# Mask and maximum of the scores: result written back to PSUM instead of a scratch tile, and both projection copies on ScalarE

## The chip, the cores and the metric

The kernel runs on one core of a Trainium2 chip. The metric is device time in microseconds for one execution of the whole program. The core has TensorE (PE, matmuls from SBUF into PSUM), VectorE (DVE), ScalarE (ACT), GpSimd (POOL) and SyncE (SP), which issues the DMAs. Each engine works through its own queue in order; semaphores order the engines against each other, and, where an instruction touches what an earlier one of the same engine wrote, also an engine against itself.

## The reference

Four layers alternate on x of 2048 rows and 640 columns: attention, Fourier, attention, Fourier. Each is applied to a layer-normalised x and added to x.

```python
def _A_ref(x, wqkv, wo):
    H = 32; Dh = D // H; W = 256
    q, k, v = ...                          # x @ wqkv, 32 heads of 20
    scores = einsum("bhqd,bhkd->bhqk", q, k) * (Dh ** -0.5)
    mask = (i - j >= 0) & (i - j < W)      # causal, a window of 256
    p = softmax(where(mask, scores, -1e9))
    return einsum("bhqk,bhkd->bhqd", p, v) @ wo
def _B_ref(x, ...):                        # real part of a 2-D DFT
    return dft_seq_re @ (x @ dft_hid_re.T) - dft_seq_im @ (x @ dft_hid_im.T)
```

All of it is float32.

## The kernel before

fp32 products are made from fp32r matmuls: each operand is split into a high part (a rounded copy) and a low part (the rest), and three products hi·hi, hi·lo, lo·hi are summed in PSUM. Splitting is what ScalarE, VectorE and GpSimd do most of the time.

An attention layer projects q and k in 10 chunks of 128 rows by 2048 columns, stores them to DRAM, and loads them back packed, four heads (a quad) at a time, into `qp` and `kp`. There are 8 quads of 16 blocks of 128 queries. `heads` walks over 128 head steps and a lead-in of 10. In a step s, t and v are three points of a pipeline that stand 10 steps and one step apart:

- `s_head` (L546): for a block of queries and each of four heads, one matmul gives the scores of 128 queries against up to 384 keys (128 in the first block of a quad, 256 in the second). The scores go to one of three PSUM banks (2, 3, 4) in turn. One VectorE instruction adds the mask to them and takes each row's maximum, which lands in a column of `mc`. The chip runs it as two instructions: the custom operation over the scores and an accumulator read that writes `mc`. Its element-wise result, masked scores, is used by nobody.
- `m_rows` (L561): every four steps the maxima are transposed, negated and stored as a 61st row of `qp`.
- `t_head` and `t_exp` (L574, L581): the scores again, transposed (keys by queries), with that 61st row subtracting the maximum, into bank 0 or 1; ScalarE takes the exponential into `pt`. `t_mask` on GpSimd zeroes what the mask excludes.
- `pv` (L600): the product with v into bank 5, one step later.

Between the two halves of a step `fill` puts other TensorE work: first the projection of the remaining chunks (`project`, `pieces`), then parts of the output product. `pieces` multiplies two sets of 512 columns in lockstep into banks 6 and 7 (in the lead-in four, with 0 and 1 as well). When a set is complete, `copied` (L470) brings each of its banks to an SBUF tile `x`; before the change the odd one goes by VectorE (L474), the even one by ScalarE (L476). GpSimd then rounds and subtracts (L477, L478) in the following half steps, and SyncE stores. The copies are issued at the end of `fill` (L685), so in each queue they stand ahead of the second half of the step.

The order is written out by the program: nothing reorders it. Only the semaphores are derived, from which tile or bank an instruction reads and writes.

Of the kernel before, what the change touches and what calls it, by code (L numbers as in the profile page):

```python
# [9 lines left out]
BF16 = mybir.dt.bfloat16  # L10
U16 = mybir.dt.uint16
AF = mybir.ActivationFunctionType
# [5 lines left out]
P = 128  # L18
# [9 lines left out]
NEG = -1.0e30  # L28
# [33 lines left out]
class Net:  # L62
    def __init__(self, nc, tc, ctx, a):
        self.nc, self.tc, self.a = nc, tc, a
        const = ctx.enter_context(tc.tile_pool(name="const", bufs=1))
        self.ln = ctx.enter_context(tc.tile_pool(name="ln", bufs=5))
        self.slots = ctx.enter_context(tc.tile_pool(name="slots", bufs=1))
        psum = ctx.enter_context(tc.tile_pool(name="psum", bufs=1, space=PSUM))
        self.work = ctx.enter_context(tc.tile_pool(name="work", bufs=2))
        dram = ctx.enter_context(tc.tile_pool(name="dram", bufs=1, space=DRAM))  # L70

        self.banks = psum.tile([P, 8, 512], F32, name="banks")

        def fixed(name, cols, dt):
            return const.tile([P, cols], dt, name=name)

        self.ident = fixed("ident", P, F32)
        nc.sync.dma_start(self.ident, a["ident"])
        self.mask = fixed("mask", 384, BF16)
        self.ux = fixed("ux", 384, BF16)  # L80
        self.ones = const.tile([1, 128], F32, name="ones")
        nc.vector.memset(self.ones, 1.0)
        self.half = fixed("half", 1, F32)
        nc.vector.memset(self.half, -0.5)
        self.big, self.home = [None] * 4, [0, 1, 2, 3]
        self.qp, self.kp = [None] * 2, [None] * 2

        self.qk = dram.tile([2, 2 * D, S], F32, name="qk_d")
        self.vd = dram.tile([NQ, P, NB, 96], F32, name="v_d")
        self.ud = dram.tile([2, KC, P, S], F32, name="u_d")  # L90
        self.od = dram.tile([H, 32, S], F32, name="o_d")
        self.rd = dram.tile([NSB, H, 512], F32, name="r_d")
        self.xs = [dram.tile([S, D], F32, name=f"x_d{i}") for i in range(3)]
        self.turn = {}
        self.xn = {}
        self.ready, self.hid = 0, False
        self.slot = None
        self.posted = {}
        self.heavy = []
        self.left = 0  # L100
        self.tmp = None
# [355 lines left out]
    def pieces(self, c, sbs, role):  # L457

        w = self.turn["w", c]
        sets, of = [], {}  # L460
        for sb in sbs:
            xt = self.xnt(sb)
            if sb % 2 == 0:
                sets.append(([], []))
            p = self.bank(role)
            of[id(p)] = p, sb, self.last_bank
            sets[-1][0].append(p)
            sets[-1][1].append([((w[:, 0, k, :], w[:, 1, k, :]), (xt[:, 0, k, :], xt[:, 1, k, :])) for k in range(KC)])

        def copied(p, sb):  # L470
            st = self.work.tile([P, 2, 512], F32R, name="c", tag="c", bufs=3)
            r = self.raw()[:, :512]
            if sb % 2:
                self.nc.vector.tensor_copy(r, p)  # L474
            else:
                self.nc.scalar.activation(r, p, AF.Copy)  # L476
            self.post(1, lambda: self.nc.gpsimd.tensor_copy(st[:, 0, :], r))  # L477
            self.post(2, lambda: self.nc.gpsimd.tensor_tensor(  # L478
                out=st[:, 1, :], in0=r, in1=st[:, 0, :].bitcast(F32), op=OP.subtract))
            self.post(6, lambda: self.store_qk(c, sb, st))  # L480
        for r in self.lockstep(sets):
            if isinstance(r, tuple):
                for p in r[1]:
                    p, sb, k = of[id(p)]
                    self.heavy.append((k, lambda p=p, sb=sb: copied(p, sb)))
                r = 0
            yield r
# [33 lines left out]
    def heads(self, xsrc, xdst, hook):  # L521
# [20 lines left out]
        def s_bank():  # L542
            turn[0] += 1
            return 2 + turn[0] % 3

        def s_head(quad, qb, z, e):  # L546

            n = min(qb + 1, 3)
            k0 = qb - n + 1
            b = 64 * e  # L550
            p = self.banks[:, s_bank(), :n * P]
            nc.tensor.matmul(  # L552
                p, qp[quad % 2][b:b + 60, z, qb * P:(qb + 1) * P],
                kp[quad % 2][b:b + 60, z, k0 * P:(qb + 1) * P], start=True, stop=True)
            if (quad, qb // 4) not in mc:
                mc[quad, qb // 4] = pool.tile([P, 2, 2, 4], F32, name="mc", tag="mc")
            nc.vector.tensor_tensor_reduce(  # L557
                out=self.ux[:, :n * P], in0=p, in1=self.mask[:, 384 - n * P:], scale=1.0, scalar=NEG,
                op0=OP.add, op1=OP.max, accum_out=mc[quad, qb // 4][:, z, e, qb % 4:qb % 4 + 1])

        def m_rows(quad, u):  # L561
# [128 lines left out]
        for step in range(-LEAD, steps + 1):  # L690
# [24 lines left out]
            for z in range(2):  # L715
                for e in range(2):
                    heads = [(t_head, t, e), (s_head, s, 1 - e)]
                    for head, n, i in heads[::-1] if e else heads:
                        if 0 <= n < steps:
                            head(n // 16, n % 16, z, i)  # L720
                if 0 <= t < steps:
                    for e in range(2):
                        t_exp(t // 16, t % 16, z, e, e + 1)
                    t_mask(t // 16, t % 16, z)
                if z:
                    if 0 <= v < steps:
                        pv(v // 16, v % 16)
                    if rows:
                        m_rows(*rows)
                if z == 0 and t >= 0 or t < -1 or t >= steps:  # L730
                    fill(nf)
                self.tick()
# [798 lines left out]
```

## Time and profile before

| what | value |
|---|---|
| median of 3 runs | 2284.34 us (2281.37 to 2285.37) |
| profiled execution | 2282.01 us, of it the span 2280.3 us |
| mean granted TensorE clock | 0.989 |
| PE busy | 2185.6 us (96%) |
| VectorE busy | 1512.0 us (66%) |
| ScalarE busy | 1106.0 us (49%) |
| GpSimd busy | 1004.1 us (44%) |
| score matmuls (L552), first and last start, first attention layer | 124.5 and 521.4 us |
| the same, second attention layer | 1255.8 and 1651.9 us |
| mask-and-maximum (L557) | 1024 instructions, 545.1 us busy, mean 532 ns; 186.5 us of idle VectorE ahead of them |

Busy time is a share of stretches with different limits, so the head steps have to be read by themselves. A matmul's end is modelled and matmuls overlap, so a PE that is busy all the time need not be at its peak; idle time of the weight loads (PEld) tells more. A wait is put down to the semaphore that came last.

### The profile page before, as it was taken

Reading aid. Unit: us, or ns where it says so; the run is one execution under the profiler, and the core shown is the slowest. Engines: PE = TensorE matmul, PEld = TensorE weight load, DVE = VectorE, ACT = ScalarE, POOL = GpSimd, SP = SyncE. Lnnn points to the kernel's source line nnn. Section 1 sums busy time; section 2 is a strip of 40 time slices with the busy share of each in tenths; the row PEclk is TensorE's granted clock in tenths of the full one; section 3 lists DMA queues with packets and bytes.
Section 4 is the critical chain, followed back from the end, with each engine's and each line's share of the span. In section 5 each row is a group of like instructions: output and inputs, shape, how many; then the busy total and the mean of one; then the engine's idle time right before and its main releaser. Section 6 shows DMA issues by size and latency. Waiting matters only on the chain.

```text
span 2280.3 us, 50212 instructions
## 1 busy us (share of the span) xinstructions
PE 2185.6 (96%) x18064; PEld 1811.8 (79%) x18064; DVE 1512.0 (66%) x3737; ACT 1106.0 (49%) x2369; POOL 1004.1 (44%) x1540
## 2 busy tenths in 40 slices
PE   8999999999889999999999999998998899999999
PEld 7976777677768888889999777766777688888999
DVE  6357777774787868772451677776746978688622
ACT  2117776666454545541331377676655545445310
POOL 3037666777743223230130566668777332332300
PEclk9999999999989999999999999999999999999999
DMA  5545656775435353655455456657654354446553
GB/s 188 179 148 181 182 175 193 226 208 162 139 116 177 121 184 130 219 173 166 153 170 182 153 184 176 192 179 227 198 174 129 115 171 148 160 151 207 165 167 99
DMA packets 217305, 385.64 MB, mean 169 GB/s; under 512 B 38880, under 2 KB 85472, under 8 KB 217056
## 3 DMA queue, kind: packets, MB, share of 16 engines
q1 hardware_dynamic: 217056, 382.43, 52.7%
q8 instruction: 143, 2.34, 0.4%
q14 instruction: 106, 0.87, 0.1%
HBM read 267.39 MB, written 113.77 MB: 167 GB/s over the span
## 4 chain that ended last, share of the span: by engine, by line
PE 36%; POOL 5%; DVE 4%; DMA 2%; issue 2%; ACT 1%; SPq 0%; DVEq 0%; POOLq 0%; ACTq 0%
PE banks L1224 14%; PE banks L171 11%; PE banks L189 4%; PE banks L607 3%; DVE ux L557 2%; PE banks L577 2%; PE banks L552 2%; POOL big L164 1%; POOL c L478 1%; POOL pt L592 0%; POOL pt L596 0%; DMA rr<-r_d 0%; POOL kp L164 0%; POOL x L773 0%; DMA kp<-qk_d 0%
## 5 line engine op out<-in xcount | busy, mean ns | idle before, releaser
L557 DVE CUSTOM_DVE_ANT_0 ux<-banks,mask 128x384 bf16<-128x384 f32 (+2 forms) x1024 | 545.1, 532 | 186.5 <-PE banks L552 53.0
L586 ACT ACTIVATE pt<-banks 128x384 f32<-128x384 f32 (+2 forms) x1024 | 435.8, 469 | 223.2 <-PE banks L552 118.5
L577 PE MATMUL banks<-qp,kp 61*128 61x384 f32 (+2 forms) x1024 | 329.7, 383 | 8.9 <-ACT pt L586 8.5
L552 PE MATMUL banks<-kp,qp 60*128 60x384 f32 (+2 forms) x1024 | 313.3, 377 | 19.5 <-DVE mc L557 18.8
L592 POOL TENSOR_SCALAR_AFFINE_SELECT pt<-pt 128x256 f32<-128x256 f32 x512 | 210.2, 411 | 224.3 <-ACT pt L586 185.9
L189 PE MATMUL banks<-big,wc 64*128 64x512 f32 x1920 | 263.0, 391 | 0.4 <-DVE pt L372 0.4
L577 PEld LDWEIGHTS banks<-qp,kp 61*128 61x128 f32 x1024 | 179.4, 185 | 68.9 <-ACT pt L586 40.0
L552 PEld LDWEIGHTS banks<-kp,qp 60*128 60x128 f32 x1024 | 172.8, 185 | 74.8 <-DVE mc L557 61.6
L607 PE MATMUL banks<-pt,vq 128*32 128x128 f32 x5760 | 217.2, 278 | 7.8 <-POOL pt L592 7.8
L164 DVE TENSOR_TENSOR qp<-pt,qp 128x512 fp32r<-128x512 f32 (+1 forms) x209 | 173.2, 837 | 50.0 <-ACT qp L158 49.0
L189 PEld LDWEIGHTS banks<-big,wc 64*128 64x128 f32 x1920 | 184.3, 186 | 20.4 <-DVE pt L372 0.5
L607 PEld LDWEIGHTS banks<-pt,vq 128*32 128x32 f32 x5760 | 144.2, 110 | 61.9 <-issue 46.7
L596 POOL TENSOR_SCALAR_AFFINE_SELECT pt<-pt 128x256 f32<-128x256 f32 x448 | 184.2, 411 | 0.0
L158 ACT ACTIVATE qp<-pt 128x512 fp32r<-128x512 f32 (+1 forms) x209 | 128.9, 624 | 102.4 <-DMA pt<-c 35.3
L1224 PE MATMUL banks<-qp,big 128*128 128x512 f32 x630 | 156.2, 399 | 6.1 <-POOL big L164 4.3
L1153 POOL TENSOR_TENSOR pt<-pt,pt 128x512 f32<-128x512 f32 x40 | 58.5, 1466 | 214.0 <-DMA pt<-c 162.4
L1412 DVE TENSOR_TENSOR x<-banks,x 128x320 f32<-128x320 f32 x64 | 29.8, 488 | 178.4 <-DMA x<-x_d 103.1
L1224 PEld LDWEIGHTS banks<-qp,big 128*128 128x128 f32 x630 | 120.3, 193 | 32.6 <-POOL big L164 5.8
L158 ACT ACTIVATE c<-pt 128x512 fp32r<-128x512 f32 x144 | 88.1, 624 | 75.7 <-DVE pt L1150 37.3
L171 PE MATMUL banks<-big,pt 128*128 128x320 f32 x768 | 118.2, 309 | 0.9 <-DVE pt L1349 0.9
L1224 PE MATMUL banks<-qp,xc 128*128 128x512 f32 x480 | 119.0, 395 | 0.0
L164 DVE TENSOR_TENSOR c<-pt,c 128x512 fp32r<-128x512 f32 x140 | 107.9, 783 | 15.1 <-ACT c L158 12.7
(202 smaller groups left out, 4395.3 us busy)
## 6 DMA issues: line engine op xcount, KB each, us to landing
pt<-c SPq DMA_DIRECT2D x188, 512.0 KB
qk_d<-c SPq DMA_DIRECT2D x80, 512.0 KB
kp<-qk_d SPq DMA_DIRECT2D x384, 80.0 KB
qp<-qk_d SPq DMA_DIRECT2D x384, 80.0 KB
kp<-u_d SPq DMA_DIRECT2D x32, 640.0 KB
o_d<-ou SPq DMA_DIRECT2D x64, 256.0 KB
x_d<-x SPq DMA_DIRECT2D x48, 320.0 KB
v_d<-pt SPq DMA_DIRECT2D x16, 768.0 KB
```

What stands on the lines that cost most here:

```text
L158: nc.scalar.activation(hi, src, AF.Copy, scale=-1.0 if neg else 1.0)
L164: (eng or nc.vector).tensor_tensor(out=lo, in0=src, in1=hi.bitcast(F32), op=OP.subtract)
L171: self.nc.tensor.matmul(p, x, y, start=n == 0, stop=n == last)
L189: self.nc.tensor.matmul(ps[a], x[r], y[r], start=half + i == 0, stop=half == 1 and i == n - 1, skip_group_check=True)
L552: nc.tensor.matmul(p, qp[quad % 2][b:b + 60, z, qb * P:(qb + 1) * P], kp[quad % 2][b:b + 60, z, k0 * P:(qb + 1) * P], start=True, stop=True)
L557: nc.vector.tensor_tensor_reduce(out=self.ux[:, :n * P], in0=p, in1=self.mask[:, 384 - n * P:], scale=1.0, scalar=NEG, op0=OP.add, op1=OP. ...
L577: nc.tensor.matmul(self.banks[:, e, :n * P], kp[quad % 2][b:b + 61, z, kb * P:(kb + 1) * P], qp[quad % 2][b:b + 61, z, kb * P:(kb + n) * P ...
L586: nc.scalar.activation(pt[quad, kb][:, 2 * z + e0:2 * z + e1, :n * P], self.banks[:, e0:e1, :n * P], AF.Exp, scale=SCALE)
L592: nc.gpsimd.affine_select(out=t[:, :, 0:P], in_=t[:, :, 0:P], pattern=[[0, 2], [1, P]], compare_op=OP.is_ge, fill=0.0, base=0, channel_mul ...
L596: nc.gpsimd.affine_select(out=t[:, :, 256:384], in_=t[:, :, 256:384], pattern=[[0, 2], [-1, P]], compare_op=OP.is_gt, fill=0.0, base=0, ch ...
L607: nc.tensor.matmul(p[32 * h:32 * h + 32, :], vq[:, 96 * (kb % 4) + 21 * h:96 * (kb % 4) + 21 * h + 32], t[:, h, (qb - kb) * P:(qb - kb + 1 ...
L1224: nc.tensor.matmul(self.banks[:, bk, :], p, b[q], start=start and m == 0, stop=stop and last and m == 2, skip_group_check=True)
```

## The change

The element-wise result of the mask-and-maximum goes back to the bank that holds the scores (in place, as fp32) instead of to `ux`, a bf16 tile in SBUF that all 1024 shared; the tile is gone. In `copied` both copies go by ScalarE.

```diff
         self.mask = fixed("mask", 384, BF16)
-        self.ux = fixed("ux", 384, BF16)
...
             r = self.raw()[:, :512]
-            if sb % 2:
-                self.nc.vector.tensor_copy(r, p)
-            else:
-                self.nc.scalar.activation(r, p, AF.Copy)
+            self.nc.scalar.activation(r, p, AF.Copy)
...
             nc.vector.tensor_tensor_reduce(
-                out=self.ux[:, :n * P], in0=p, in1=self.mask[:, 384 - n * P:], scale=1.0, scalar=NEG,
+                out=p, in0=p, in1=self.mask[:, 384 - n * P:], scale=1.0, scalar=NEG,
                 op0=OP.add, op1=OP.max, accum_out=mc[quad, qb // 4][:, z, e, qb % 4:qb % 4 + 1])
```

VectorE in the steady head steps, around one projection copy, before. Rows `ISA ux,mc` are the mask-and-maximum, rows `ISA mc` its accumulator read; in brackets stand the semaphores that an instruction waits for, by the engine that raises them (DVE is VectorE's own).

```order
L557 ISA ux,mc<-banks,mask 128x384 [waits DVE_49,PE_49]
L557 ISA mc 128x1
L557 ISA ux,mc<-banks,mask 128x384 [waits DVE_49,PE_49]
L557 ISA mc 128x1
L474 COPY x<-banks 128x512 [waits PE_49,Pool_49]
L557 ISA ux,mc<-banks,mask 128x384 [waits DVE_49,PE_49,Activation_49]
L557 ISA mc 128x1
L557 ISA ux,mc<-banks,mask 128x384 [waits DVE_49,PE_49]
```

The same place after the change, where the lines are four lower:

```order
L553 ISA banks,mc<-banks,mask 128x384 [waits PE_49]
L553 ISA mc 128x1
L553 ISA banks,mc<-banks,mask 128x384 [waits PE_49]
L553 ISA mc 128x1
L553 ISA banks,mc<-banks,mask 128x384 [waits PE_49,Activation_49]
L553 ISA mc 128x1
L553 ISA banks,mc<-banks,mask 128x384 [waits PE_49]
```

The copy is gone from VectorE's queue, and with `ux` the wait of each mask-and-maximum for its own engine; the wait for TensorE stays.

ScalarE at a copy of the same kind, before. L586 are the exponentials, four to a step, two in each half; L616 and L566 bring products and maxima out of PSUM, L158 rounds weights.

```order
L616 ACTIVATE ou_98<-banks 128x256
L566 ACTIVATE mt<-banks 16x128
L586 ACTIVATE pt_97<-banks 128x384 x2
L476 ACTIVATE x<-banks 128x512
L586 ACTIVATE pt_97<-banks 128x384 x2
L586 ACTIVATE pt_94<-banks 128x384 x2
L158 ACTIVATE wc<-x 128x384
```

And after:

```order
L612 ACTIVATE ou_97<-banks 128x256
L562 ACTIVATE mt<-banks 16x128
L582 ACTIVATE pt_96<-banks 128x384 x2
L472 ACTIVATE x<-banks 128x512 x2
L582 ACTIVATE pt_96<-banks 128x384 x2
L582 ACTIVATE pt_93<-banks 128x384 x2
L157 ACTIVATE wc<-x 128x384
```

Two copies now stand between the exponentials of the first and the second half of that step. The order of TensorE, GpSimd and SyncE is what it was; in 6 places, three in each lead-in, a projection matmul gains a wait for ScalarE, where VectorE's copy had been covered by a wait of an earlier matmul.

## The prediction

> **What bounds the kernel now.** I read the page first, then busy time in stretches of the span, then the list of waits, then the order of time on VectorE, ScalarE and TensorE inside two head steps.
>
> ```profile
> span 2280.3 us, 50212 instructions
> ```
>
> Busy time by stretch: the stretch, its length, then busy us and count of instructions of each engine, the granted clock, the DMA share.
>
> ```profile
> core 0: us, PE busy (x) PEld busy (x) DVE busy (x) ACT busy (x) POOL busy (x), PEclk, DMA share, GB/s
> 125.00:160.00 35.00, 34.76 (x308) 28.34 (x309) 21.26 (x77) 3.65 (x8) 13.54 (x16) 1.00 0.39 123
> 200.00:240.00 40.00, 39.03 (x535) 28.59 (x533) 30.90 (x117) 27.81 (x69) 27.05 (x61) 1.00 0.62 192
> ...
> 800.00:1180.00 380.00, 377.80 (x2061) 338.50 (x2060) 237.10 (x387) 154.04 (x267) 97.16 (x77) 1.00 0.53 174
> ```
>
> The first row is the lead-in of the head steps, the second a steady part of them, the third the Fourier layer, which the change does not touch. In the steady part PE looks full, yet its weight loads are busy for 28.6 of 40 us against 338.5 of 380 in the Fourier layer: PE waits there between a load and its matmul. The list of waits names for whom:
>
> ```profile
> PEld banks L552 <- DVE mc L557: 61.6, 175, 1.0
> ...
> PE banks L552 <- DVE mc L557: 18.8, 63, 0.8
> ```
>
> The score matmul (L552) waits for the mask-and-maximum (L557) to give a PSUM bank back. The next fence is VectorE in order of time in two steady head steps (start us, length us):
>
> ```profile
> 302.98 0.56 DVE L557 CUSTOM_DVE_ANT_0 ux<-banks,mask 128x384 bf16<-128x384 f32 x1
> 303.46 0.08 DVE L557 DVE_READ_ACCUMULATOR2_ANT mc<- 128x1 f32 x1
> 303.46 0.25 DVE L630 RECIPROCAL rc<-sm 128x16 f32<-128x16 f32 x1
> 303.69 0.56 DVE L557 CUSTOM_DVE_ANT_0 ux<-banks,mask 128x384 bf16<-128x384 f32 x1
> 304.17 0.08 DVE L557 DVE_READ_ACCUMULATOR2_ANT mc<- 128x1 f32 x1
> 304.40 0.56 DVE L557 CUSTOM_DVE_ANT_0 ux<-banks,mask 128x384 bf16<-128x384 f32 x1
> ```
>
> One mask-and-maximum starts every 0.71 us (303.69, 304.40). Its accumulator read starts after 0.48 us, and from there 0.23 us pass before the next one. In that hole a RECIPROCAL of 0.25 us fits without moving the next start, so VectorE could have worked; it was waiting. Four of them make 2.84 us a step.
>
> One quad of steady steps, cut at the first transposed matmul (L577) of its steps 0, 1, 2, 3, 4 (to 5), 6, 7 (to 9), 10, 11, 12 (to 13), 14 (to 15); columns as above:
>
> ```profile
> 302.88:305.50 2.62, 2.62 (x45) 2.02 (x41) 2.24 (x8) 1.69 (x4) 0.93 (x3) 1.00 0.45 145
> 305.50:307.89 2.39, 2.39 (x29) 1.61 (x25) 1.87 (x8) 1.86 (x6) 1.54 (x4) 1.00 0.65 170
> 307.89:311.14 3.25, 3.19 (x37) 2.05 (x33) 2.62 (x9) 2.23 (x6) 1.54 (x4) 1.00 0.61 195
> 311.14:314.34 3.20, 2.93 (x39) 2.08 (x38) 2.77 (x10) 2.48 (x7) 1.85 (x5) 1.00 0.14 42
> 314.34:320.83 6.49, 6.10 (x84) 4.37 (x80) 4.99 (x20) 4.92 (x12) 6.49 (x12) 1.00 0.59 177
> 320.83:323.66 2.83, 2.83 (x43) 2.20 (x41) 1.68 (x10) 1.81 (x5) 2.83 (x8) 1.00 0.97 355
> 323.66:331.53 7.87, 7.87 (x119) 6.00 (x118) 5.76 (x22) 6.00 (x15) 4.60 (x13) 1.00 0.55 157
> 331.53:334.46 2.93, 2.93 (x45) 2.08 (x41) 2.35 (x10) 1.88 (x6) 1.63 (x5) 1.00 0.72 155
> 334.46:337.42 2.96, 2.69 (x39) 1.95 (x38) 2.53 (x10) 2.47 (x7) 1.72 (x5) 1.00 0.18 60
> 337.42:343.14 5.72, 5.72 (x84) 4.23 (x80) 4.71 (x18) 4.24 (x10) 5.72 (x11) 1.00 0.70 219
> 343.14:349.10 5.96, 5.68 (x83) 4.22 (x79) 4.76 (x18) 2.85 (x10) 2.66 (x8) 1.00 0.75 264
> ```
>
> Where VectorE has slack (step 0, and 7 to 9, after the narrow instructions of 128 and 256 columns) a step takes 2.62 us: TensorE's own pace. Elsewhere three things stretch it. VectorE does in steps 2, 10, 14 and 15. GpSimd is busy 6.49 of 6.49, 2.83 of 2.83 and 5.72 of 5.72 us in steps 4 to 6 and 12 to 13, where it cuts the projection pieces. The copies fall in steps 3 and 11. So VectorE paces only a part of what it makes others wait for.
>
> **The change part by part.** The rows for its prices:
>
> ```profile
> L557 DVE CUSTOM_DVE_ANT_0 ux<-banks,mask x1024: 280/558/560, 125.1 to 1653.4; 128x384 bf16<-128x384 f32 x149, 128x128 bf16<-128x128 f32 x11, 128x256 bf16<-128x256 f32 x11
> ...
> L557 DVEq EVENT_SEMAPHORE  x1022: 21/21/1487, 125.4 to 1653.3; - x171
> ...
> L1150 DVE TENSOR_TENSOR pt<-pt 128x512 f32<-128x512 f32 x60 | 42.1, 702 | 0.0
> ...
> L474 DVE COPY x<-banks x32: 685/689/693, 136.6 to 1559.9; 128x512 f32<-128x512 f32 x32
> ...
> L476 ACT ACTIVATE x<-banks x32: 597/598/601, 136.6 to 1559.8; 128x512 f32<-128x512 f32 x32
> ```
>
> *The scratch tile goes, and a wait with it.* All 1024 instructions wrote the one tile `ux`, so each waited for the one before it on its own engine; 1022 extra semaphore instructions carried that wait. Written into the scores' own bank the outputs no longer overlap, and the wait on TensorE alone is left. The next one may then start where the RECIPROCAL did, at the accumulator read: 0.48 us instead of 0.71, four in 1.93 us. VectorE falls clear of the 2.62 us of TensorE, and more saving on it would buy nothing.
>
> *The output goes to PSUM as fp32.* No row shows VectorE writing PSUM. The nearest rows show reading: a 512-column copy out of PSUM takes 689 ns, an operation of that width within SBUF 702. From below I bound the price at nothing (0 ns, no gain either, since the columns are streamed anyway); from above at a second pass over the columns. A pass costs (558 - 280) / 256 = 1.09 ns a column, so 0.42 us for 384, and 0.90 us from start to start. I take the lower end, since as a source PSUM is no slower than SBUF.
>
> *The copies.* 32 of 689 ns leave VectorE, 32 of 598 ns come to ScalarE. Eight lie in the lead-in, where ScalarE is busy 3.65 of 35 us. There the change adds six waits of projection matmuls (with all of TensorE's queue behind them) for ScalarE. Between a set's end and the next use of its banks lies the other set:
>
> ```profile
> 136.59 1.99 PE L189 MATMUL banks<-big,wc 64*128 64x512 f32 x16
> ...
> 138.59 1.77 PE L189 MATMUL banks<-big,wc 64*128 64x512 f32 x14
> ```
>
> That is 3.8 us, and two copies end 1.2 us after their set. So I cost it at nothing; were that cover gone, it would be at most 0.6 us in each of six places, 3.6 in all. The other 24 stand right behind the 24 that are there, in steps 3 and 11, with two exponentials of the same step queued after them. Step 11 now: ScalarE, TensorE, VectorE:
>
> ```profile
> 336.42 0.60 ACT L476 ACTIVATE x<-banks 128x512 f32<-128x512 f32 x1 [0.18 <-PE banks L189]
> 336.92 0.87 ACT L586 ACTIVATE pt<-banks 128x384 f32<-128x384 f32 x2
> ...
> 336.22 0.34 PE L577 MATMUL banks<-qp,kp 61*128 61x384 f32 x1
> ...
> 337.45 0.44 PE L577 MATMUL banks<-qp,kp 61*128 61x384 f32 x1
> ...
> 336.53 0.69 DVE L474 COPY x<-banks 128x512 f32<-128x512 f32 x1
> ```
>
> The scores of 336.22 are there at 336.56, but their exponential starts at 336.92, behind the copy, and ends about half of 0.87 us later, just before the next transposed matmul at 337.45 needs its bank. Another 0.60 us of copy puts that matmul 0.60 later. Nothing covers it, so steps 3 and 11 come to 2.62 + 0.60 = 3.22 us. GpSimd's cutting of the second piece waits for its copy, which ends at 337.6 either way (336.87 + 0.69, or 336.42 + 1.20); GpSimd's full stretches stay.
>
> *The sum for one quad* (46.22 us now): step 2 gives 3.25 - 2.62 = 0.63, step 10 gives 0.31, steps 14 and 15 give 5.96 - 5.24 = 0.72. In steps 12 and 13 GpSimd is full but TensorE shows no idle time (5.72 of 5.72), so I take half of 5.72 - 5.24, 0.25. Step 3 stays, step 11 costs 0.26, the rest stays. Together 1.65 us.
>
> ```profile
> PEld banks L552 <- DVE mc L557: 19.2, 60, 0.5
> ...
> 455.96:459.90 3.94, 3.67 (x53) 2.76 (x52) 2.62 (x11) 2.25 (x8) 3.80 (x6) 1.00 0.92 226
> ...
> 462.98:467.29 4.31, 3.65 (x56) 2.76 (x52) 2.87 (x11) 2.65 (x6) 4.31 (x8) 1.00 0.78 202
> ```
>
> The first row is the same wait between 205.0 and 446.7 us, 5.2 quads: 3.7 us each. So 1.65 of 3.7, 45%, comes back. The later head steps, filled with output products, are alike: the long ones (3.94 and 4.31 us) have GpSimd busy 3.80 and 4.31. I apply the 45% to all 61.6 us: 28 us. The profiled execution took 2282.0 us (2280.3 span, 1.7 around it), 2.3 below the median of 2284.3; 2282.0 - 28 = 2254, from the median 2256. I say 2255.
>
> **The rivals.**
>
> *All of the wait returns.* GpSimd's full stretches could be a backlog that shrinks when masks come earlier, and ScalarE's second copy could slide into its gaps. For it: ScalarE is busy 27.8 of 40 us. Against it: the three stretches at 100%. Time: 2282 - 61.6 = 2220.
>
> *The hole stays.* VectorE may need the time to finish an instruction, wait or no wait. The RECIPROCAL at 303.46 speaks against it, though it is another operation than the one that would follow now. Then only copies leave VectorE, at most 0.6 us in each of 24 places where ScalarE costs about the same: 0 to -7 us, 2279. The Trainium skill says this in "VectorE: DVE Perf Modes", section "The DRAIN you can't avoid": the next operation starts only when the pipe is empty, and eight copies took 13.88 us with a semaphore after each and with one after the last alike. By that rule the sum would be 2279; the trace disagrees with it in the row at 303.46, and I leave it a chance for that reason only.
>
> *Slower: PSUM takes the write at half pace.* At 0.90 us a start, a quad has 14 steps of 3.6, one of 4 x 0.63 and one of 4 x 0.34 (the 256- and 128-column forms with their second pass): 54.3 us on VectorE alone, 8.1 more than 46.2. Seven such quads in each of two layers: +113, so 2395. The point from which it decides is a start-to-start time of 0.71 us, 0.23 more than now lies between a start and its accumulator read. Nothing in the trace shows a PSUM operand doing that.
>
> **How the numbers follow.** The forecast has 0.57, all the wait 0.20, the hole that stays 0.13, slower 0.10. The likeliest gives 2255. The range takes in the two middle rivals, 2220 to 2281, and leaves the slow one out. About 0.2% (4.6 us) is what a measurement can tell from no change; the rival of the hole straddles it. So faster 0.83, the same 0.07, slower 0.10.
>
> **What would show it.** Right: mask-and-maximum starts 0.48 us apart when scores are ready; the semaphore instructions of that line down from 1022 to some tens; the 61.6 us wait under 15; steps 2, 10, 14 and 15 at 2.6 us; 64 copies of 598 ns on ScalarE, and the transposed matmul waiting for exponentials in steps 3 and 11. Wrong: a start-to-start time still at 0.71 (the hole stays), an instruction near 0.98 us long (the PSUM write), steps 4 to 6 shorter than 9.3 us together (GpSimd was no bound, and the gain is larger), or a granted clock under 1.00 in 200 to 400 us as TensorE fills up.

## The result, and the profile after

The changed kernel takes 2262.28 us (median; 2256.79 to 2264.44) against 2284.64 us before (2281.37 to 2285.37) on the same chip: a ratio of 0.9901, with a 95% interval of 0.988 to 0.9923, or 22 us less. The forecast was 28 us less. The profiled execution took 2260.54 us.

The mask-and-maximum and the copies, by line (duration ns as least/median/most):

```profile
span 2258.8 us, 49233 instructions
...
L553 DVE CUSTOM_DVE_ANT_0 banks<-banks,mask x1024: 289/567/602, 126.6 to 1633.5; 128x384 f32<-128x384 f32 x149, 128x128 f32<-128x128 f32 x11, 128x256 f32<-128x256 f32 x11
L553 DVE DVE_READ_ACCUMULATOR2_ANT mc<- x1024: 133/141/146, 126.8 to 1634.0; 128x1 f32 x171
L553 DVEq EVENT_SEMAPHORE  x58: 21/21/21, 176.1 to 1624.4; - x58
...
L472 ACT ACTIVATE x<-banks 128x512 f32<-128x512 f32 x64 | 34.7, 595 | 55.6 <-PE banks L188 24.1 <-POOL wc L163 17.8 <-issue 12.5
```

VectorE in order of time in a steady head step (start us, length us):

```profile
300.67 0.57 DVE L553 CUSTOM_DVE_ANT_0 banks<-banks,mask 128x384 f32<-128x384 f32 x1
301.15 0.14 DVE L553 DVE_READ_ACCUMULATOR2_ANT mc<- 128x1 f32 x1
301.15 0.60 DVE L553 CUSTOM_DVE_ANT_0 banks<-banks,mask 128x384 f32<-128x384 f32 x1
```

The hole is gone: the next mask-and-maximum starts at the accumulator read of the one before, 0.48 us after its start (300.67, 301.15) instead of 0.71. The semaphore instructions fell from 1022 to 58. Writing fp32 to PSUM shows in two durations: the accumulator read takes 141 ns instead of 83, beside the next instruction, and the instruction itself 567 instead of 558 (medians). Neither moves the next start. What TensorE waits for:

```profile
PEld banks L573 <- ACT pt L582: 43.9, 141, 0.8
...
PEld banks L548 <- DVE mc L553: 23.6, 51, 3.0
...
PE banks L548 <- DVE mc L553: 10.7, 17, 2.7
```

The waits of the score matmul for the mask-and-maximum fell from 61.6 and 18.8 us to 23.6 and 10.7. Its longest grew from 1.0 to 3.0; that one comes up again below.

Now the steady quad, cut at its steps as in the prediction (2, 3, 4 to 5, 6, 10, 11, 12 to 13, 14 to 15 are shown):

```profile
303.87:306.77 2.90, 2.90 (x34) 2.21 (x34) 2.55 (x10) 2.05 (x6) 1.53 (x4) 1.00 0.71 212
306.77:309.82 3.05, 2.69 (x39) 1.94 (x39) 2.64 (x11) 2.85 (x9) 2.28 (x6) 1.00 0.37 117
309.82:316.03 6.21, 5.88 (x81) 4.50 (x82) 4.60 (x17) 4.92 (x12) 6.12 (x11) 1.00 0.56 169
316.03:318.85 2.82, 2.82 (x43) 2.17 (x41) 1.21 (x8) 1.81 (x5) 2.82 (x8) 1.00 1.01 376
...
326.73:329.57 2.84, 2.84 (x45) 2.15 (x41) 2.48 (x10) 1.87 (x6) 1.54 (x5) 1.00 0.61 172
329.57:332.46 2.89, 2.70 (x40) 1.92 (x39) 2.43 (x11) 2.81 (x8) 2.10 (x6) 1.00 0.13 39
332.46:337.91 5.45, 5.45 (x80) 4.35 (x80) 4.31 (x16) 4.13 (x10) 5.45 (x10) 1.00 0.69 216
337.91:342.98 5.07, 5.07 (x83) 4.03 (x80) 4.44 (x17) 2.90 (x11) 2.66 (x8) 1.00 0.92 320
```

Steps 2, 4 to 5, 12 to 13 and 14 to 15 are shorter; steps 3 and 11, with two copies on ScalarE, still take 3.05 and 2.89. This quad takes 44.1 us instead of 46.2. All quads of the two attention layers, as quad 0, quads 1 to 4, quads 5 to 7; before:

```profile
161.25:209.67 48.42, 44.83 (x590) 32.19 (x589) 36.92 (x136) 32.17 (x79) 34.40 (x73) 1.00 0.65 206
209.67:395.75 186.08, 180.55 (x2452) 131.02 (x2448) 145.16 (x536) 130.20 (x320) 126.24 (x281) 1.00 0.59 183
395.75:550.88 155.13, 146.49 (x2091) 113.96 (x2088) 102.25 (x358) 102.34 (x247) 114.44 (x219) 0.98 0.67 195
1291.89:1339.89 48.00, 44.82 (x590) 32.15 (x590) 36.92 (x136) 32.17 (x79) 34.40 (x73) 1.00 0.65 207
1339.89:1525.59 185.70, 180.69 (x2453) 131.20 (x2450) 145.06 (x536) 130.36 (x320) 126.00 (x280) 1.00 0.60 183
1525.59:1681.11 155.52, 146.15 (x2091) 114.02 (x2087) 102.31 (x358) 102.51 (x247) 114.76 (x219) 0.98 0.65 195
```

And after:

```profile
162.81:210.74 47.93, 44.75 (x589) 33.49 (x588) 35.66 (x135) 32.85 (x81) 34.25 (x73) 0.96 0.63 206
210.74:387.05 176.31, 172.38 (x2453) 132.38 (x2450) 141.10 (x529) 131.62 (x328) 125.98 (x281) 1.00 0.61 189
387.05:545.93 158.88, 149.82 (x2091) 116.96 (x2088) 100.79 (x356) 102.96 (x249) 114.46 (x219) 0.95 0.67 195
1284.11:1330.74 46.63, 43.40 (x590) 32.65 (x590) 35.66 (x135) 32.68 (x81) 34.35 (x73) 1.00 0.67 209
1330.74:1506.89 176.15, 172.26 (x2453) 132.34 (x2449) 141.10 (x529) 131.54 (x328) 125.97 (x281) 1.00 0.62 193
1506.89:1661.90 155.01, 148.43 (x2092) 116.02 (x2088) 100.58 (x356) 103.03 (x249) 114.44 (x219) 0.96 0.67 196
```

Of 21.5 us of span, quads 1 to 4 give 9.8 and 9.6, quad 0 gives 0.5 and 1.4, and 3.6 lie outside the quads. Quads 5 to 7 give nothing: +3.75 and -0.5. So there are three questions: what the PSUM result and the copies are each worth, what holds the steps that did not come down to 2.62 us, and why the late quads gained nothing.

### The profile page after: what moved, and what is told of

It is laid out like the page before. It is cut to its first block, busy times and chain, and to the rows that moved or that the text cites. A ratio compares the mean times of both kernels' runs of the same rounds, so it can differ in the third digit from the quotient of the medians.

```text
span 2258.8 us, 49233 instructions
## 1 busy us (share of the span) xinstructions
PE 2169.5 (96%) x18064; PEld 1817.8 (80%) x18064; DVE 1489.8 (66%) x3705; ACT 1114.2 (49%) x2401; POOL 1014.9 (45%) x1540
## 3 DMA queue, kind: packets, MB, share of 16 engines
q8 instruction: 143, 2.34, 0.5%
## 5 line engine op out<-in xcount | busy, mean ns | idle before, releaser
L553 DVE CUSTOM_DVE_ANT_0 banks<-banks,mask 128x384 f32<-128x384 f32 (+2 forms) x1024 | 526.7, 557 | 174.7 <-PE banks L548 125.7
L582 ACT ACTIVATE pt<-banks 128x384 f32<-128x384 f32 (+2 forms) x1024 | 430.8, 469 | 209.4 <-PE banks L548 115.0
L573 PE MATMUL banks<-qp,kp 61*128 61x384 f32 (+2 forms) x1024 | 320.0, 376 | 10.7 <-ACT pt L582 9.2
L548 PE MATMUL banks<-kp,qp 60*128 60x384 f32 (+2 forms) x1024 | 285.5, 367 | 11.4 <-DVE mc L553 10.7
L163 DVE TENSOR_TENSOR qp<-pt,qp 128x512 fp32r<-128x512 f32 (+1 forms) x209 | 167.7, 811 | 50.8 <-ACT qp L157 50.0
L548 PEld LDWEIGHTS banks<-kp,qp 60*128 60x128 f32 x1024 | 164.8, 188 | 32.9 <-DVE mc L553 23.6
L553 DVE DVE_READ_ACCUMULATOR2_ANT mc<- 128x1 f32 x1024 | 144.9, 141 | 0.0
```

The lines of the kernel that those rows point to most:

```text
L163: (eng or nc.vector).tensor_tensor(out=lo, in0=src, in1=hi.bitcast(F32), op=OP.subtract)
L548: nc.tensor.matmul(p, qp[quad % 2][b:b + 60, z, qb * P:(qb + 1) * P], kp[quad % 2][b:b + 60, z, k0 * P:(qb + 1) * P], start=True, stop=True)
L553: nc.vector.tensor_tensor_reduce(out=p, in0=p, in1=self.mask[:, 384 - n * P:], scale=1.0, scalar=NEG, op0=OP.add, op1=OP.max, accum_out=mc ...
L573: nc.tensor.matmul(self.banks[:, e, :n * P], kp[quad % 2][b:b + 61, z, kb * P:(kb + 1) * P], qp[quad % 2][b:b + 61, z, kb * P:(kb + n) * P ...
L582: nc.scalar.activation(pt[quad, kb][:, 2 * z + e0:2 * z + e1, :n * P], self.banks[:, e0:e1, :n * P], AF.Exp, scale=SCALE)
```

## The experiments

Theory: the gain is the own-engine wait on the scratch tile; the copies on ScalarE give part of it back in steps 3 and 11; GpSimd holds what is left. Rivals: it is the target PSUM that counts, or the copies pay for themselves. Each time below is a median; the ratio behind it is to runs of the kernel before on the same chip.

### One part at a time

The PSUM result alone, with the copies as before (the diff without its part in `copied`).

> Only the result goes back to PSUM; the two copies stay on VectorE and ScalarE as before. My theory (the wait on VectorE's own engine made the hole, and the second copy on ScalarE costs time in steps 3 and 11): mask-and-maximum 0.48 us apart as with the whole change, steps 3 and 11 at 2.7 instead of 3.05 and 2.87 us, so about 10 us less than the whole change, 2252. Rival (taking copies off VectorE was half of the gain): 2273.

Measured: 2256.85 us, 0.9892 (0.9878 to 0.9906). Quads 1 to 4 take 43.67 us on average.

The copies alone (the diff's part in `copied`, nothing else).

> Only the copies move to ScalarE; the scratch tile stays. My theory: mask-and-maximum still 0.71 us apart, VectorE gains 0.6 us in 24 places and TensorE waits longer for exponentials in the same steps: 2280, between 2274 and 2286. Rival (the copies were half of the gain): 2273.

Measured: 2282.28 us, 0.9995 (0.9986 to 1.0004). The copy steps 3 and 11, with the PSUM result alone:

```profile
303.20:305.82 2.62, 2.62 (x40) 1.95 (x39) 2.41 (x8) 2.43 (x8) 1.85 (x5) 1.00 0.31 96
...
325.86:328.48 2.62, 2.62 (x39) 1.91 (x39) 2.22 (x10) 2.54 (x7) 1.85 (x5) 1.00 0.15 55
```

and with the copies alone:

```profile
311.54:315.22 3.68, 3.00 (x41) 2.08 (x40) 2.93 (x11) 2.96 (x8) 2.35 (x6) 1.00 0.16 48
335.09:338.54 3.45, 2.76 (x39) 1.93 (x38) 2.71 (x9) 2.96 (x8) 2.22 (x6) 1.00 0.29 96
```

The PSUM result carries the whole gain. With one copy on each engine steps 3 and 11 come down to TensorE's 2.62 us; two on ScalarE keep them above it in both kernels. By its steady quads the change would have done better without its second half: they take 44.06 us on average with it, 0.39 more than without. That is 3 us in eight quads, and the times themselves do not tell the two kernels apart (0.9901 and 0.9892, with overlapping intervals).

### Is it PSUM, or the wait?

The copies as in the change, but the result stays in SBUF, and in quads 0 to 4 two tiles alternate, so that no instruction overwrites what the one just ahead of it wrote:

```diff
+            ux = self.rr[2].bitcast(BF16) if quad < 5 and e else self.ux
             nc.vector.tensor_tensor_reduce(
-                out=self.ux[:, :n * P], ...
+                out=ux[:, :n * P], ...
```

> Copies on ScalarE; the result goes to SBUF as before, but in the first five quads of each attention layer to two tiles in turn (ux and rr), so that no instruction has to wait for the one just before it; the last three quads have ux alone. My theory: the wait is the cause, PSUM only the means: starts at most 0.55 us apart in those five quads and steady quads of 44.0 to 44.3 us as with the whole change (before 46.2), accumulator reads of 83 ns instead of 141; from the sixth quad on as before; in all 2262 to 2268. Rival (VectorE starts early only because it writes to PSUM): 0.71 us apart, quads of 46, 2280.

Measured: 2262.39 us, 0.9914 (0.9901 to 0.9928), as the change. VectorE, and the semaphore instructions of that line:

```profile
300.52 0.56 DVE L555 CUSTOM_DVE_ANT_0 rr<-banks,mask 128x384 bf16<-128x384 f32 x1 [0.24 <-PE banks L575]
301.00 0.08 DVE L555 DVE_READ_ACCUMULATOR2_ANT mc<- 128x1 f32 x1
301.00 0.55 DVE L555 CUSTOM_DVE_ANT_0 ux<-banks,mask 128x384 bf16<-128x384 f32 x1
...
L555 DVEq EVENT_SEMAPHORE  x944: 21/21/865, 126.0 to 1632.4; - x189
```

Starts 0.48 us apart without any write to PSUM, and with 944 semaphore instructions still there. In the last quads of the same run, where `ux` is alone again, they are 0.71 apart:

```profile
453.11 0.56 DVE L555 CUSTOM_DVE_ANT_0 ux<-banks,mask 128x384 bf16<-128x384 f32 x1
...
453.82 0.56 DVE L555 CUSTOM_DVE_ANT_0 ux<-banks,mask 128x384 bf16<-128x384 f32 x1
```

So neither the target nor the number of semaphore instructions counts, but the wait for the instruction directly ahead. It cost 0.71 - 0.48 = 0.23 us each time. (The wait and a write to the same tile directly ahead always go together here; no run has the one without the other.) The accumulator read is back at 0.08 us, so the 58 ns more are what the PSUM target adds.

### The other way round: both copies on VectorE

```diff
-            if sb % 2: ... else: ...
+            self.nc.vector.tensor_copy(r, p)
```

with the PSUM result.

> Result to PSUM, both copies on VectorE. My theory: VectorE has 0.7 us to spare in a step of 2.62 us, so two copies of 0.60 in steps 3 and 11 delay score matmuls a little, but exponentials come on time: between the whole change and the copies as before, 2252 to 2260. Rival (ScalarE's copies cost nothing, GpSimd sets these steps): 2262, as with the whole change.

Measured: 2263.52 us, 0.9916 (0.9903 to 0.9929): a miss. It is the rival's time, but not for the rival's reason: steps 3 and 11 are at 2.62. The steps after them, 4 and 12, come to:

```profile
314.33:317.63 3.30, 2.90 (x45) 2.01 (x41) 3.28 (x13) 2.21 (x6) 3.30 (x6) 1.00 0.49 158
337.18:340.37 3.19, 2.87 (x44) 2.00 (x40) 3.18 (x13) 1.78 (x4) 3.19 (x6) 1.00 0.46 151
```

VectorE was busy for 2.73 of 2.76 us of step 4 with the PSUM result alone; here the second copy runs into that step and VectorE has 3.28 of 3.30. TensorE's weight load waits 0.7 us in it for the mask-and-maximum, where it did not wait before. (GpSimd is full in these rows too, but it is as full with the PSUM result alone, in a step of 2.76.) So both copies on one engine cost time, whichever engine it is.

### What holds the rest: GpSimd's cutting

With the PSUM result alone, step 5 takes 3.75 us with GpSimd busy for all of it. First, both subtractions (L478) on VectorE:

```diff
-            self.post(2, lambda: self.nc.gpsimd.tensor_tensor(
+            self.post(3, lambda: self.nc.vector.tensor_tensor(
```

> Result to PSUM, copies as before, and the subtraction of the projection pieces (1.3 us each on GpSimd) on VectorE, one tick later. My theory (GpSimd's cutting sets steps 4 and 5 and part of 12 and 13, now that VectorE has time): steps 4 and 5 fall from 2.75 + 3.75 to about 2.6 + 2.7 us, 13 from 2.90 to 2.6, so 1.5 us in each of six quads in two layers, 18 us below the run with PSUM alone: 2239. Rival (a full GpSimd there is a backlog that nothing waits for): 2257, no change.

Measured: 2285.0 us, 1.0016 (1.0005 to 1.0026): a bad miss. From the waits of that kernel:

```profile
PEld banks L551 <- DVE mc L556: 69.0, 80, 6.2
...
DVE c L477 <- POOL c L476: 19.0, 4, 5.5
```

A subtraction whose rounding GpSimd has not done yet stops VectorE for up to 5.5 us, and every mask-and-maximum behind it in the queue. Nearly all of the loss lies in the two lead-ins, from the first score matmul to the first transposed one: they take 50.4 and 49.8 us, against 36.8 and 36.2 with the PSUM result alone. The steady quads lose little (44.3 against 43.67 us). Then the same place measured by itself: the subtraction is replaced by a cheaper rounding copy on GpSimd.

```diff
-            self.post(2, lambda: self.nc.gpsimd.tensor_tensor(
-                out=st[:, 1, :], in0=r, in1=st[:, 0, :].bitcast(F32), op=OP.subtract))
+            self.post(2, lambda: self.nc.gpsimd.tensor_copy(st[:, 1, :], r))
```

> PSUM alone, and the subtraction of the projection pieces (1.30 us on GpSimd) replaced by a rounding copy there (0.61 us): the low part of q and k is left out, a copy of the high part stands in its place, so the time is read with 1.4 us less of GpSimd work per pair and everything else in its place. My theory (GpSimd's cutting sets steps 4 and 5 and delays 13): step 5 falls from 3.75 to about 2.7 us and 13 from 2.90 to 2.62, 1.3 us a quad, 12 quads: 16 us below PSUM alone, 2241. Rival (a full GpSimd is only a backlog): no change, 2257.

Measured: 2240.45 us, 0.9811 (0.9795 to 0.9827). Step 5 with the subtraction and with the copy in its place:

```profile
308.58:312.33 3.75, 3.03 (x45) 2.19 (x42) 2.56 (x10) 2.46 (x7) 3.75 (x8) 1.00 0.56 174
```

```profile
303.59:306.22 2.63, 2.63 (x45) 2.07 (x42) 2.27 (x9) 2.41 (x7) 2.63 (x7) 1.00 0.72 192
```

So GpSimd does set step 5. Steps 5 and 13 fell as expected, by 1.12 and 0.26 us, 1.36 in the mean of quads 1 to 4. That the time came out at the 2241 expected is partly luck. In the profiled executions, which are 10.9 us apart where the medians are 16.4, quads 1 to 4 of both layers give 10.9 us, the two quads 0 give 8.2 where 2.6 were expected, and quads 5 to 7 take 3.3 more. A version that computes everything follows: one subtraction of two on VectorE, a tick later than there and not in the lead-in, so that its rounding is done.

```diff
+            own = sb % 2 and not self.lead
-            self.post(2, lambda: self.nc.gpsimd.tensor_tensor(
+            self.post(4 if own else 2, lambda: (self.nc.vector if own else self.nc.gpsimd).tensor_tensor(
```

> PSUM alone, and of each pair of pieces one subtraction goes to VectorE, two ticks later, outside the lead-in only. My theory: GpSimd loses 1.3 us per pair, VectorE gets 0.75 and does not wait for GpSimd any more as it did for 9.5 us of a lead-in with both subtractions: step 5 comes to 3.0, and 3 to 9 us below PSUM alone, 2248 to 2254. Rival (any subtraction on VectorE holds up the score banks behind it): 2257 or more.

Measured: 2252.4 us, 0.9863 (0.9849 to 0.9876), as expected, with step 5 at 2.94: the fastest kernel here that does all of the work, 10 us below the change. Step lengths of quad 3 of the second attention layer in these kernels (us; the fences show quad 3 of the first; steps 0, 1 and 7 to 9 stay at 2.6, 2.4 and 2.6, but for step 9 before, 2.87):

| kernel | 2 | 3 | 4 | 5 | 6 | 10 | 11 | 12 | 13 | 14 | 15 |
|---|---|---|---|---|---|---|---|---|---|---|---|
| before | 3.24 | 3.20 | 2.87 | 3.63 | 2.84 | 3.05 | 2.97 | 2.88 | 2.84 | 3.05 | 2.91 |
| the change | 2.81 | 3.05 | 2.82 | 3.39 | 2.83 | 2.83 | 2.86 | 2.84 | 2.63 | 2.77 | 2.33 |
| copies alone | 3.26 | 3.68 | 2.82 | 3.40 | 2.83 | 2.93 | 3.46 | 2.82 | 2.62 | 2.77 | 2.92 |
| PSUM result alone | 2.79 | 2.62 | 2.75 | 3.75 | 2.83 | 2.83 | 2.62 | 2.62 | 2.90 | 2.72 | 2.33 |
| cheaper cut | 2.79 | 2.62 | 2.75 | 2.62 | 2.83 | 2.83 | 2.63 | 2.63 | 2.63 | 2.74 | 2.32 |
| one low part on VectorE | 2.81 | 2.62 | 2.75 | 2.94 | 2.84 | 2.83 | 2.62 | 2.63 | 2.81 | 2.71 | 2.34 |

Steps 2, 6, 10 and 14 stay at 2.7 to 2.8 in every kernel of this table without the tile. They come every four steps, as `m_rows` does, whose transposing matmul takes 0.28 us; they are 0.1 to 0.2 us above 2.62. That it is `m_rows` fits, but was not measured by itself. Step 6 was never GpSimd's: the cheaper cut leaves it at 2.83.

### The late quads

In order of time, VectorE after the change in quad 6, at the longest wait of all (3.0 us, above):

```profile
451.78 0.14 DVE L553 DVE_READ_ACCUMULATOR2_ANT mc<- 128x1 f32 x1
455.50 0.25 DVE L626 RECIPROCAL rc<-sm 128x16 f32<-128x16 f32 x1 [3.58 <-DMA sm<-ou]
455.67 0.54 DVE L553 CUSTOM_DVE_ANT_0 banks<-banks,mask 128x384 f32<-128x384 f32 x1
```

ScalarE's last copy of what that load moves, and the load's issue on SyncE:

```profile
441.50 0.38 ACT L612 ACTIVATE ou<-banks 128x256 f32<-128x256 f32 x1
```

```profile
452.00 0.62 SPq L623 DMA_DIRECT2D sm<-ou  x1
```

The softmax sums are ready at 441.9, but their load is issued at 452.0, behind the others in SyncE's queue; the reciprocal stands in VectorE's queue for it, and TensorE waits for the mask-and-maximum behind that. The reciprocals' waits add up to 2.1 us before and 10.7 after. Postponing the reciprocal by two ticks (with the PSUM result alone):

```diff
-            at = (2, 7, 9) if quad < NQ - 1 else (1, 5, 6)
+            at = (2, 9, 11) if quad < NQ - 1 else (1, 5, 6)
```

> Result to PSUM, copies as before, reciprocals and their stores two ticks (one step) later in all quads but the last. My theory (with shorter steps the reciprocal reaches VectorE before the sums have landed, and holds all maxima behind it, 4 to 11 us in all): VectorE's wait for these sums falls under 1 us and the time by 2 to 6 us against PSUM alone, 2251 to 2255. Rival (the landing is late in single executions only, and the later store delays the output products as much): 2257, give or take 3.

Measured: 2258.19 us, 0.9891 (0.9877 to 0.9904), no different from the PSUM result alone, and so the rival's time. But the wait did not fall under 1 us: it is 6.2, against 4.5 with the PSUM result alone, so this run does not show what the kernel would do without it. In the profiled executions quad 5 is 7.2 us shorter in both layers together (45.9 and 46.2 us), quads 6 and 7 give 2.9 back, and what lies outside the quads is 9 us longer: from the first layer's last transposed score matmul to the second layer's first score matmul 706.0 us pass, against 701.8. That fits the rival's later output products, in one execution each. The same together with both subtractions on VectorE:

> The two edits of the runs before together. Both theories: 2235. GpSimd alone: 2239; the reciprocal alone: 2253; neither: 2257.

Measured: 2283.09 us, 1.0006 (0.9997 to 1.0015): the two lead-ins, at 50.4 and 51.2 us, cover everything. Next, the load is issued by ScalarE, which has just written the sums, once on the fastest kernel and once on the change:

```diff
-            self.post(at[0], lambda: nc.sync.dma_start(sm, ou[0:P:32, :]))
+            self.post(at[0], lambda: nc.scalar.dma_start(sm, ou[0:P:32, :]))
```

> As e9 (PSUM, copies as before, one subtraction of a pair on VectorE), and the load of the sums that the reciprocal reads is issued by ScalarE instead of SyncE. My theory (with shorter steps SyncE's queue falls behind, the sums' load is issued up to 9.7 us after they are there, and the reciprocal holds up VectorE, 16 us in e9): the wait for these sums falls under 3 us; as part of it would come back in other waits of the late steps, 2240 to 2248. Rival (the late steps are bound elsewhere, by loads of the output product): the wait goes and the time stays, 2252.

> The change as it is, and the load of the sums issued by ScalarE. My theory: its 10.7 us of waiting for the sums fall under 3, and the time to 2254 to 2259. Rival (bound elsewhere): 2262.

Measured: 2379.78 us, 1.0429 (1.0412 to 1.0446), and 2393.65 us, 1.0486 (1.0471 to 1.05). Both fail badly. The reciprocal waits no more, but now SyncE does; on the change (line, what it waits for, us, times, longest):

```profile
SPq L505 <- DMA sm<-ou: 117.4, 32, 6.6
SPq L564 <- DMA sm<-ou: 45.7, 14, 5.8
```

SyncE holds its own issues, the store of the maxima (L564) among them, until ScalarE's load has landed; TensorE then waits 89.7 us for the 61st row. So this made a new wait and does not settle what the late quads would do without the old one.

The last suspect is TensorE's clock. In the changed kernel's quads it stands at half speed for 34 us, in the one before for 13.6 (in quads 5 to 7 alone 30.7 and 13.6). Around the longest of these stretches, after:

```profile
420.70:424.10 3.40, 1.94 (x32) 1.07 (x24) 1.69 (x8) 2.57 (x6) 3.40 (x7) 1.00 0.78 238
...
424.10:437.80 13.70, 13.23 (x125) 9.35 (x129) 7.46 (x27) 6.83 (x18) 10.12 (x16) 0.50 0.72 230
```

TensorE is busy 1.94 of 3.40 us, and then the clock is at 0.50 for 13.7. These are the steps of quad 5 in which no filler is ready. On the fastest kernel, dummy products were put there:

```diff
+                if r is None and done[0] >= total and not made[0]:
+                    relieve()
+                    for _ in range(8):
+                        nc.tensor.matmul(self.banks[:, 6, :P], self.ident, self.ident, start=True, stop=True)
```

> This is the kernel with the PSUM result, the projection copies as before and one low part on VectorE (2252.4 us), with 24 dummy products of the identity with itself added per attention layer, 8 in each of steps 12 to 14 of quad 5, where no filler is ready; their result is not read and nothing is left out. Theory (TensorE's clock is halved after a stretch in which it has little to do, and these steps are that stretch): the half-clock interval at the end of quad 5, 10.2 us in the first attention layer and as long in the second without the dummies, goes to 3.4 us or to nothing, and the time to 2246 to 2250. Rival (the half clock has another cause, and the dummies only lengthen TensorE's queue): the interval stays at 10.2 us, and the time is 2252 or more.

Measured: 2252.28 us, 0.9858 (0.9831 to 0.9885), against 0.9863 without the dummies. The same stretch without them, then with them:

```profile
414.70:418.10 3.40, 2.01 (x32) 1.27 (x32) 3.29 (x13) 2.07 (x5) 3.13 (x6) 0.99 0.59 173
...
418.10:428.30 10.20, 10.03 (x99) 7.28 (x101) 5.46 (x21) 5.31 (x15) 7.38 (x11) 0.50 0.95 316
```

```profile
407.90:418.10 10.20, 10.18 (x148) 7.80 (x151) 7.71 (x29) 6.87 (x17) 8.92 (x19) 1.00 0.84 203
418.10:428.30 10.20, 10.20 (x136) 8.29 (x127) 6.75 (x25) 5.50 (x17) 8.76 (x13) 1.00 0.84 252
```

Half of this expectation held and half fell. The half clock follows TensorE's idleness: kept busy, TensorE keeps the full clock, in both layers. But the time did not move. Quad 5 gained 0.7 and 2.2 us; in the first layer quad 6 took 2.9 more, where VectorE still waits for the sums (3.7 us) and another half-clock stretch follows that wait. With 27.2 us of half clock in quads 5 to 7 these take 315.0 us in both layers together, with 13.6 us they take 314.1. So the half clock marks a wait there more than it causes the loss.

Quads 5 to 7 of both layers take 310.7 us before, 313.9 after, 310.0 with the PSUM result alone, 313.3 with the cheaper cut. Whatever quads 0 to 4 gain, up to 33 us with the cheaper cut in quads 1 to 4, these gain nothing; only the two kernels with the later reciprocal have them shorter (305.7 and 305.8), and those were no faster. The kernel with two scratch tiles tells most: in these quads it has one tile and its wait, and they take 310.7 us, as before. So there the scratch tile's wait is not what sets the time. That the sums' load is late is seen in them; that it, and nothing else, sets their time was not shown, and it stays open.

## Why the prediction was right, and where it was not

**The wait of the scratch tile** was read rightly: 0.48 us from start to start, by the RECIPROCAL row that had slipped into the hole. The alternating tiles show that the wait alone did it. So the rival in which the hole stays is disproved: without a wait on the instruction ahead, the next starts at 0.48 of a 0.56 us instruction, and a wait costs 0.23 us rather than nothing. The rule that the prediction took from the Trainium skill's "VectorE: DVE Perf Modes", section "The DRAIN you can't avoid", that the next operation starts only when the pipe is empty and a semaphore costs nothing extra, does not hold for this operation; the same section adds that a next operation that is not held starts earlier, and that is what is seen here.

**The PSUM write at its lower bound of nothing** was right: 58 ns more on the accumulator read and 9 on the instruction, no longer spacing. So was the price of nothing for the six new waits in the lead-ins: these take 36.8 and 36.2 us, 0.1 more each.

**The sum for one quad** was 1.65 us and came to 2.1 in the quad shown, 2.4 as a mean (19.3 us over eight quads). Its steps were off both ways. Steps 2 and 10 came to 2.8 or 2.9 instead of 2.62, most likely since the floor of 2.62 left out `m_rows`. Steps 14 and 15 were sized at 5.24 together and took 5.07 to 5.10, step 15 going below that floor. Steps 3 and 11 were to be 3.22 and are 3.05 and 2.89, so step 11 gained 0.07 where it was to lose 0.26. Steps 4 and 5 fell by 0.28 and were to stay. That steps 3 and 11 stay above 2.62 because of the copies was right, and the copies alone show it at 3.68 and 3.46.

**GpSimd as the bound of steps 4 to 6 and 12 to 13** was right for step 5 and, less, for step 13; for the others the full GpSimd row misled. Step 6 has its 2.83 us without GpSimd's load too, step 4 its 2.75 with the cheaper cut and without it, and step 12 comes down to 2.62 with GpSimd still full. One of the prediction's own signs of being wrong came true here: steps 4 to 6 took 6.21 + 2.82 = 9.03 us, under the 9.3 that it had named.

**A slip in the working.** GpSimd's second piece was said to find its copy done at 337.6 either way, with VectorE's copy starting at 336.87. The quoted row has it start at 336.53, so it ended at 337.22, and two copies on ScalarE end 0.4 us later. It did not change the sum, since GpSimd's full stretches shrank all the same.

**The step that failed** is the last one: 45% of the wait applied to all 61.6 us. Quads 1 to 4 were sized at 13.2 us (8 times 1.65) and gave 19.3; everything else in the 28 us, 14.8, was to come mainly from the later head steps, "alike" to the steady ones, and quads 5 to 7 took 3.2 more. Two errors of opposite sign left 22 for 28, so that the total came near is partly luck. The weight loads' wait shows where the steps are not alike: it fell from 31.7 to 1.4 us in quads 1 to 4, and went from 18.8 to 19.3 in quads 5 to 7. The two long late steps quoted for that step, 3.94 and 4.31 us, became 3.81 and 4.99. In "what would show it", the wait under 15 us was missed for the same reason (23.6).

**The clock** was named as what would make it wrong in 200 to 400 us. It stayed at 1.00 there; it fell before that, for 3.4 us in quad 0, and from quad 5 on.

## What to carry to other kernels

A tile that nobody reads is not free when every instruction of a queue writes it: look for semaphore instructions as many as the instructions themselves, see whether the wait is for the instruction directly ahead, and give the writes two places in turn. Price a change by stretches of the program that have been cut open, and let a stretch that was not cut keep its time in the sum until its own rows say otherwise. When an operation moves to another engine's queue, ask when its operand is ready there: one subtraction of two, a tick later, gained 4 us; both, a tick earlier and in the lead-in as well, lost 28, of them 27 in the lead-ins.

## What the runs showed of the hardware

The granted clock goes to 0.50 in stretches of 3.4 us or a multiple of it (3.4, 6.8, 10.2, 13.7). Cutting the head steps of four kernels (before, the change, one low part on VectorE, dummies) into 3.41 us windows in step with these stretches, 17 windows at full clock have TensorE busy for less than 65%, and 15 of them are followed by a half-clock one; of the 920 at 65% or more, one is. So here a stretch in which TensorE is busy half of the time was mostly enough. The Trainium skill's "TensorE: Matmul & The Clock Gate", section "Part 1: The HAM clock gate (the "warmup" mystery)", tells of a free-running window of about 3.4 us after which an idle array is throttled. The lengths here agree; the busy share at which it happens comes from these rows.

A load issued from ScalarE's queue made SyncE's queue wait for its landing, 163 us at two lines together in the changed kernel, though SyncE's issues before had no such wait to speak of. Why the two queues are tied was not tried further.
